# Attention and two feed-forward layers on one core: probability tiles, early loads and the spread of work on W in the first batch

## The chip, the cores and the metric

The kernel runs on one core of a Trainium2 chip. The metric is the device time of one execution in microseconds (us), lower is better. The kernel before takes 925.04 us, the median of three runs (924.96 to 925.62).

The core has engines with instruction streams of their own: PE (TensorE, matrix products and transposes through it; PEld is its loading of weights), DVE (VectorE), ACT (ScalarE), POOL (GpSimd) and SP (SyncE), which here issues all DMAs. Each works through its own stream in a fixed order and meets the others at semaphores.

## The reference

Windowed attention over 4 batches, 8 heads, 576 positions and head width 64, and behind it two feed-forward layers without a softmax or norm in between:

```python
def _attn_ref(q, k, v):                     # q, k, v: (4, 8, 576, 64)
    scores = scale * np.matmul(q, k.transpose(0, 1, 3, 2))
    mask = (rel >= 0) & (rel < 128)          # rel = query position - key position
    scores = np.where(mask, scores + slopes * -abs(rel), -1e9)
    attn = np.exp(scores - max)
    attn = attn / (sum(attn) + 1e-9)
    return np.matmul(attn, v)
x = attention, heads side by side            # (2304, 512)
h = ((x @ w1) * (x @ w2)) @ w3               # 512 -> 1024 -> 1024
y = h @ w_out                                # 1024 -> 512
h = y @ w_in                                 # 512 -> 2048
out = (h * clip(h + 3, 0, 6) / 6) @ v_out    # 2048 -> 512
```

## The kernel before

**Stages.** The first feed-forward layer uses the product W = w3 @ w_out, which the kernel makes itself while the attention of the first batch runs. After that come four batches of `ab` units (x @ w1 times x @ w2, line 464) and `y` units (times W, line 482), with the attention of the next batch between them, and then the second layer (`h_unit`, `o_unit`, lines 585 and 605). Products that need more than one pass are made of three matrix products of split operands (`mm3`, line 46).

**Attention.** It goes by head pairs n = 0 to 15, four to a batch. A pair takes six slots (`attn_slot`, line 304). Slot 0: the second head's product with v of the pair before (`pv(n - 1, 1)`), and the first two score tiles; slot 1: normalising these two, two more score tiles; slot 2: the fifth score tile (`j = 4`, the tail), normalising the rest; slot 3 and 4: transposes of the probabilities of the first and second head (`pt`), operands q and k of the next pair, loads of q and k for the pair behind it; slot 5: `pv(n, 0)`. A score tile j goes PE (line 193, or 195 and 196) to DVE (bias and row minimum, line 207) to ACT (exp, line 216) to DVE (1/sum, lines 224 and 225) to POOL (normalise, line 232) to PE (`pt`, lines 250 and 254), then ACT or DVE copies `th` (lines 260, 262) and PE multiplies by v (line 277). The result `xf` is split into `xh` and `xl` (line 298), which `ab` needs from all four pairs of the batch. Pairs 0 to 3 are "whole": q, k, v are used unsplit in buffers that alternate by `n % 2`; from pair 4 on they are split (`t_q`, `t_k`, `t_v`).

**Probability tiles.** Tiles `pr` of score tiles 0 to 3 come from one ring of four buffers (line 201), which is one pair's worth. The tail has one fixed tile `prt`. Ring `tl` of four buffers of the same size serves split pairs alone (line 241).

**Work on W.** w_out comes in four loads of 1 MB (`wo`), w3 in eight (`w3`), and w1 and w2 in eight (`w12`, f = 0 to 7). Each is unpacked by one ACT and two DVE instructions (`unpack`, lines 60 to 63). For each w3 load two halves of four products follow (`w_half`, line 389, tile `wps`), in unsplit f32, each product two instructions in the trace. `w12_unit` splits further (lines 69 and 70). Raw loads pass through three buffers, two in `rawp` and one in `rawx`. The list `work` (line 427) has 32 items: four `wo`, then each w3 with its two halves, with `w12` 0 to 3 ahead of the last three w3. Units `w12` 4 to 7 stand behind the whole list (lines 450 to 455), since their split tiles take the memory of unpacked w_out, and their loads reuse `rawp`.

**Order.** The program order of the first stage is the loop over 26 slots: `attn_slot(s)` and behind it the work items up to a share of the list:

```python
nslot = SLOTS * NP + 2          # 26
WEND = 6
upto = (s + 1) * len(work) // (nslot - WEND)
```

With `WEND = 6` all 32 items stand by slot 19, and slots 20 to 25 have attention alone. The order on each engine isn't this program order: the kernel is built with `schedule_with_timeline_sim=True` (line 694), and a planner fixes each engine's order beforehand, by its own estimate of when each instruction could run; among those it takes as ready, the one that stands first in the program goes first. On the chip that order is kept.

Of the kernel before, what the change touches and what calls it, by code (L numbers as in the profile page):

```python
# [8 lines left out]
F32 = mybir.dt.float32  # L9
# [8 lines left out]
P = 128  # L18
B, H, S, D = 4, 8, 576, 64
# [3 lines left out]
def tile_attention_moe_moe2(ctx: ExitStack, tc: tile.TileContext, qT, kT, vm, vt, wo, w3, w12, w2x, out):  # L23
# [7 lines left out]
    nc = tc.nc  # L31
# [6 lines left out]
    NHP = B * NP  # L38
# [51 lines left out]
    a1 = apool_ctx.enter_context(tc.tile_pool(name="a1", bufs=1, side="right"))  # L90
# [11 lines left out]
    def whole(n):  # L102
        return n < NWHOLE
# [2 lines left out]
    kw = [a1.tile([P, 2 * S], F32, tag=t, name=f"kw{t}") for t in ("rawk", "kh")]  # L106
    vw = [a1.tile([P, NC, P], F32, tag=t, name=f"vw{t}") for t in ("rawv", "vs")]
    rel8 = a1.tile([P, H, 2 * P], BF16, tag="kl", name="rel8")
    prt = a1.tile([P, 2 * P], F32, name="prt")
    sp1 = {}  # L110

    def split_tiles():
        if not sp1:
            sp1["rawq"] = a1.tile([P, 2 * S], F32, tag="rawq", name="rawq")
            sp1["rawk"] = a1.tile([P, 2 * S], F32, tag="rawk", name="rawk")
            sp1["rawv"] = a1.tile([P, NC, P], F32, tag="rawv", name="rawv")
            sp1["qs"] = a1.tile([P, SQ], F32R, tag="qs", name="qs")
            sp1["kh"] = a1.tile([P, 2 * S], F32R, tag="kh", name="kh")
            sp1["kl"] = a1.tile([P, 2 * S], F32R, tag="kl", name="kl")
            sp1["vs"] = a1.tile([P, NC, 2, P], F32R, tag="vs", name="vs")  # L120
            nc.gpsimd.memset(f32(sp1["qs"][:, 2 * S : SQ]), 0.0)
            nc.gpsimd.memset(sp1["rawv"][D:P, NC - 1, :], 0.0)
        return sp1

    def load_hp(n, names):
        for nm in names:
            if nm == "v":
                r = vw[n % 2] if whole(n) else split_tiles()["rawv"]
                nc.sync.dma_start(out=r[:, 0 : NC - 1, :], in_=vm[n])
                nc.sync.dma_start(out=r[0:TAIL, NC - 1, :], in_=vt[n])  # L130
                continue
            src = qT if nm == "q" else kT
            if whole(n):
                r = (qw if nm == "q" else kw)[n % 2]
            else:
                r = split_tiles()["raw" + nm]
            for a in range(1 if whole(n) else 2):
                nc.sync.dma_start(out=r[a * D : (a + 1) * D, 0 : 2 * S], in_=src[n])

    def slope(n, h):  # L140
        return 2.0 ** (-8.0 * (2 * (n % NP) + h + 1) / H)

    def t_q(n):

        if whole(n):
            return
        r, qs = split_tiles()["rawq"], split_tiles()["qs"]
        for h in range(2):
            sc = -(float(D) ** -0.5) / slope(n, h)
            c = slice(h * S, (h + 1) * S)  # L150
            nc.scalar.activation(qs[:, c], r[:, c], AF.Copy, scale=sc)
            nc.vector.scalar_tensor_tensor(
                out=qs[D:P, c], in0=r[D:P, c], scalar=sc, in1=f32(qs[D:P, c]), op0=ALU.mult, op1=ALU.subtract
            )
# [8 lines left out]
    def t_v(n):  # L163

        if whole(n):
            return
        t = split_tiles()
        r = t["rawv"].rearrange("p c (h d) -> p c h d", h=2)
        vs = t["vs"].rearrange("p c h (t d) -> p c h t d", t=2)
        for h in range(2):  # L170
            nc.vector.tensor_copy(vs[:, :, h, 0, :], r[:, :, h, :])
            nc.gpsimd.tensor_tensor(
                out=vs[:, :, h, 1, :], in0=r[:, :, h, :], in1=f32(vs[:, :, h, 0, :]), op=ALU.subtract
            )
# [6 lines left out]
    def scores(n, j):  # L181
        k0 = max(0, P * (j - 1))
        nk = min(S, P * (j + 1)) - k0
        mo = P if j == 0 else 0
        tail = j == NC - 1
        m = TAIL if tail else P
        ps = ps_s.tile([P, 2, 2 * P], F32, tag="s", name=f"s_{n}_{j}")
        for h in range(2):
            o = ps[:, h, 0:nk]
            qc = slice(h * S + P * j, h * S + P * (j + 1))  # L190
            kc = slice(h * S + k0, h * S + k0 + nk)
            if whole(n):
                nc.tensor.matmul(o, qw[n % 2][:, qc], kw[n % 2][:, kc], start=True, stop=True)
            else:
                nc.tensor.matmul(o, sp1["qs"][:, qc], sp1["kh"][:, kc], start=True, stop=False)
                nc.tensor.matmul(o, sp1["qs"][:, qc], sp1["kl"][:, kc], start=False, stop=True)

        if j == 0:
            stat[n] = [a1.tile([P, 2 * NC], F32, tag=t, bufs=2, name=f"{t}_{n}") for t in ("mn", "sm", "rc")]
        mn, sm, _ = stat[n]  # L200
        pr = prt if tail else a1.tile([P, 2, 2 * P], F32, tag="pr", bufs=4, name=f"pr_{n}_{j}")
        for h in range(2):
            a = h * m if tail else 0
            o = pr[a : a + m, 0:nk] if tail else pr[:, h, 0:nk]
            col = 2 * j + (0 if tail else h)

            nc.vector.tensor_tensor_reduce(
                out=o, in0=ps[0:m, h, 0:nk],
                in1=rel8[0:m, 2 * (n % NP) + h, mo : mo + nk] if whole(n) else relm[0:m, mo : mo + nk],
                op0=ALU.add, op1=ALU.min, scale=-(float(D) ** -0.5) if whole(n) else slope(n, h), scalar=3.0e38,  # L210
                accum_out=mn[a : a + m, col : col + 1],
            )
        for h in range(1 if tail else 2):
            o = pr[:, 0:nk] if tail else pr[:, h, 0:nk]
            col = 2 * j + h
            nc.scalar.activation(
                o, o, AF.Exp, bias=mn[:, col : col + 1], scale=-1.0, accum_out=sm[:, col : col + 1]
            )
        prob[n, j] = pr

    def normalize(n, js):
        _, sm, rc = stat[n]
        c0, c1 = 2 * js[0], min(2 * js[-1] + 2, 2 * NC - 1)
        nc.vector.tensor_scalar_add(rc[:, c0:c1], sm[:, c0:c1], 1e-9)
        nc.vector.reciprocal(rc[:, c0:c1], rc[:, c0:c1])  # L225
        for j in js:
            tail = j == NC - 1
            k0 = max(0, P * (j - 1))
            nk = min(S, P * (j + 1)) - k0
            for h in range(1 if tail else 2):  # L230
                o = prob[n, j][:, 0:nk] if tail else prob[n, j][:, h, 0:nk]
                nc.gpsimd.tensor_scalar(  # L232
                    out=o, in0=o, scalar1=rc[:, 2 * j + h : 2 * j + h + 1], scalar2=1.0, op0=ALU.mult, op1=ALU.mult
                )
# [69 lines left out]
    def attn_slot(g):  # L304
        n, s = divmod(g, SLOTS)
        ok = 0 <= n < NHP
        if s == 0:
            if 1 <= n <= NHP:
                pv(n - 1, 1)
            if ok:  # L310
                scores(n, 0)
                scores(n, 1)
        if not ok and not (s in (3, 4) and n == -1):
            return
        if s == 1:
            normalize(n, (0, 1))
            if n > 0 and whole(n - 1):
                load_hp(n, "v")
            scores(n, 2)
            scores(n, 3)  # L320
        elif s == 2:
            scores(n, 4)
            t_v(n)
            if n + 1 < NHP and not whole(n):
                load_hp(n + 1, "v")
            normalize(n, (2, 3, 4))
        elif s == 3:
            if ok:
                pt(n, 0, 0)
                pt(n, 0, 1)  # L330
            if n + 1 < NHP:
                t_q(n + 1)
                if n + 2 < NHP:
                    load_hp(n + 2, "q")
        elif s == 4:
            if ok:
                pt(n, 1, 0)
                pt(n, 1, 1)
            if n + 1 < NHP:
                t_k(n + 1)  # L340
                if n + 2 < NHP:
                    load_hp(n + 2, "k")
        elif s == 5:
            if ok:
                pv(n, 0)
# [60 lines left out]
    make_identity(nc, ident)  # L406
    for t in vw:
        nc.gpsimd.memset(t[D:P, NC - 1, :], 0.0)
    nc.gpsimd.memset(prt[:, P + D :], 0.0)
    nc.gpsimd.memset(three, 3.0)  # L410
    queue = [("wo", i) for i in range(KH)] + [("w3", i) for i in range(KF)]
    queue[-3:-3] = [("w12", f) for f in range(KH)]
# [2 lines left out]
    def more():  # L415
        nonlocal nxt
        if nxt < len(queue):
            k, i = queue[nxt]
            load((k, i), {"wo": wo, "w3": w3, "w12": w12}[k][i], rawp, rawp, rawx)
            nxt += 1  # L420

    more()
    load_hp(0, "v")
    more()
    load_hp(1, "qk")
    more()
    work = []
    for k, i in queue:
        work += [(k, i)] + ([("h", i, 0), ("h", i, 1)] if k == "w3" else [])
    nslot = SLOTS * NP + 2  # L430
    WEND = 6

    def do_work(w):
        if w[0] == "h":
# [7 lines left out]
    for s in range(nslot):  # L442
        attn_slot(s)
        upto = (s + 1) * len(work) // (nslot - WEND)
        if wi < len(work) and upto >= len(work):
# [253 lines left out]
```

## Time and profile before

| | us |
|---|---|
| median of three runs | 925.04 |
| the profiled execution, whole time | 920.97 |
| its span, first to last instruction | 919.1 |
| PE busy in it | 891.5 |

The profiled execution is 4.07 us faster than the median. All rows are from it; 1.87 us of its own time lie outside the span. Times of rows count from the span's start. In a timeline row the first two numbers are start and length of a merged run of instructions, and the bracket tells how long the engine was idle before it and what ended that. PE's lengths are modelled ends and overlap their successors.

### The profile page before, as it was taken

The page shows a single profiled execution, that of the slowest core. Times are in us where ns is not written, and L with a number is a line of the kernel's source. Part 1 is how long each engine was busy: PE and PEld are TensorE (multiplying, and loading weights), DVE is VectorE, ACT ScalarE, POOL GpSimd, SP SyncE. Part 2 cuts the span into 40 slices and gives each one's busy share as a digit, 9 for nine tenths or more (in the row PEclk, how much of TensorE's full clock was granted, in tenths as well). Part 3 has the DMA queues.
Part 4 walks back from the last instruction along what each step waited for, and adds up shares of the span by engine and source line. Part 5 has one row for each costly group of instructions (what it writes and reads, how often), then busy time and mean ns, then how long its engine had stood idle before and what let it go on. Part 6 is the DMA issues. An engine that isn't in the chain of part 4 may idle for free.

```text
span 919.1 us, 13413 instructions
## 1 busy us (share of the span) xinstructions
PE 891.5 (97%) x5216; PEld 782.5 (85%) x5216; DVE 439.6 (48%) x935; ACT 402.2 (44%) x856; POOL 152.0 (17%) x225
## 2 busy tenths in 40 slices
PE   5999889999999999999999999999999999999997
PEld 4555679999999999999899888888888888888896
DVE  5784767566664746554617683232223222322232
ACT  6664656565565635554416572232232222222232
POOL 4321323322232323230200010020001001000000
PEclk9999889999999999999999999999999999999999
DMA  9973422321322232103505651010001000100000
GB/s 290 357 267 115 157 66 65 80 68 48 84 73 59 66 85 66 39 2 117 185 27 188 234 200 47 0 69 1 1 0 46 1 1 1 46 1 1 15 32 24
DMA packets 23151, 74.00 MB, mean 81 GB/s; under 512 B 2864, under 2 KB 8496, under 8 KB 18480
## 3 DMA queue, kind: packets, MB, share of 16 engines
q1 hardware_dynamic: 23088, 73.15, 25.2%
q8 instruction: 41, 0.67, 0.3%
q14 instruction: 22, 0.18, 0.1%
HBM read 63.70 MB, written 9.44 MB: 80 GB/s over the span
## 4 chain that ended last, share of the span: by engine, by line
PE 89%; DMA 4%; DVE 3%; ACT 1%; issue 1%; POOL 1%; SPq 0%; DVEq 0%; ACTq 0%; POOLq 0%
PE o L47 7%; PE o L49 7%; PE o L48 7%; PE h L47 7%; PE h L48 7%; PE h L49 7%; PE ab L47 7%; PE ab L48 7%; PE ab L49 7%; PE wps L389 6%; PE X L277 4%; PE y L47 3%; PE y L48 3%; PE y L49 3%; DMA rawv<-in_w2x_dram 3%; PE pt L250 3%
## 5 line engine op out<-in xcount | busy, mean ns | idle before, releaser
L47 PE MATMUL ab<-xh,w12h 128*128 128x288 f32 x512 | 156.4, 306 | 5.0 <-ACT xh L69 3.1
L48 PE MATMUL ab<-xl,w12h 128*128 128x288 f32 x512 | 152.7, 298 | 0.0
L49 PE MATMUL ab<-xh,w12l 128*128 128x288 f32 x512 | 152.6, 298 | 0.0
L599 DVE SCALAR_TENSOR_TENSOR rl<-rl,h 128x512 f32<-128x512 f32 (+1 forms) x80 | 50.6, 634 | 208.7 <-ACT rl L598 208.7
L598 ACT ACTIVATE rl<-h,three 128x512 f32<-128x512 f32 (+1 forms) x80 | 51.6, 647 | 211.6 <-PE h L49 210.9
L47 PE MATMUL h<-yh,v2h 128*128 128x512 f32 (+1 forms) x320 | 118.5, 370 | 2.2 <-DVE rl L599 2.2
L49 PE MATMUL h<-yh,v2l 128*128 128x512 f32 (+1 forms) x320 | 118.1, 369 | 0.0
L48 PE MATMUL h<-yl,v2h 128*128 128x512 f32 (+1 forms) x320 | 117.9, 369 | 0.0
L47 PE MATMUL o<-v2h,g2h 128*128 128x512 f32 x288 | 112.9, 392 | 0.0
L48 PE MATMUL o<-v2l,g2h 128*128 128x512 f32 x288 | 112.3, 390 | 0.0
L49 PE MATMUL o<-v2h,g2l 128*128 128x512 f32 x288 | 111.4, 391 | 0.0
L47 PEld LDWEIGHTS ab<-xh,w12h 128*128 128x128 f32 x512 | 96.9, 190 | 7.1 <-ACT xh L69 3.5
L48 PEld LDWEIGHTS ab<-xl,w12h 128*128 128x128 f32 x512 | 97.5, 190 | 0.5 <-issue 0.2
L49 PEld LDWEIGHTS ab<-xh,w12l 128*128 128x128 f32 x512 | 97.3, 190 | 0.0
L232 POOL TENSOR_SCALAR pr<-pr,rc 128x256 f32<-128x256 f32 (+1 forms) x128 | 66.8, 541 | 153.6 <-DVE rc L225 77.5
L545 POOL TENSOR_TENSOR yl<-yraw,yh 128x1024 fp32r<-128x1024 f32 (+1 forms) x10 | 23.3, 2351 | 331.6 <-ACT yh L544 331.6
L70 DVE TENSOR_TENSOR g2l<-rl,g2h 128x512 fp32r<-128x512 f32 (+1 forms) x80 | 54.7, 684 | 47.3 <-ACT g2h L69 47.1
L47 PE MATMUL y<-g,Wh 128*128 128x288 f32 x256 | 75.6, 299 | 0.0
L48 PE MATMUL y<-g,Wh 128*128 128x288 f32 x256 | 75.4, 297 | 0.0
L49 PE MATMUL y<-g,Wl 128*128 128x288 f32 x256 | 75.0, 295 | 0.0
L47 PEld LDWEIGHTS h<-yh,v2h 128*128 128x128 f32 x320 | 60.1, 188 | 13.4 <-DVE rl L599 2.6
L48 PEld LDWEIGHTS h<-yl,v2h 128*128 128x128 f32 x320 | 60.1, 188 | 11.0
(106 smaller groups left out, 1645.9 us busy)
## 6 DMA issues: line engine op xcount, KB each, us to landing
raww<-in_w_dram SPq DMA_DIRECT2D x16, 1024.0 KB, 5.9
rawv<-in_w2x_dram SPq DMA_DIRECT2D x16, 1024.0 KB, 4.8
rawq<-in_qT_dram SPq DMA_DIRECT2D x24, 288.0 KB, 4.4
rawk<-in_kT_dram SPq DMA_DIRECT2D x24, 288.0 KB, 4.9
yT<-yf SPq DMA_DIRECT2D x32, 144.0 KB, 2.3
out_dram<-ob SPq DMA_DIRECT2D x18, 256.0 KB, 2.0
rawwo<-in_wo_dram SPq DMA_DIRECT2D x4, 1024.0 KB, 10.2
yraw<-yT SPq DMA_DIRECT2D x4, 1024.0 KB, 5.2
```

The costliest lines, as they stand in the source:

```text
L47: nc.tensor.matmul(ps, lh, rh, start=first, stop=False)
L48: nc.tensor.matmul(ps, lh, rl, start=False, stop=False)
L49: nc.tensor.matmul(ps, ll, rh, start=False, stop=last)
L70: lo_eng.tensor_tensor(out=lo, in0=src, in1=f32(hi), op=ALU.subtract)
L232: nc.gpsimd.tensor_scalar(out=o, in0=o, scalar1=rc[:, 2 * j + h : 2 * j + h + 1], scalar2=1.0, op0=ALU.mult, op1=ALU.mult)
L250: nc.tensor.transpose(ps[:, o : o + P], prob[n, j][:, h, c : c + P], ident)
L277: nc.tensor.matmul(X[:, c0 : c0 + nq], l, r, start=bank not in seen, stop=last[bank] == idx, skip_group_check=True)
L389: nc.tensor.matmul(ps[:, 0:DM], w3v[i][:, m, :], wov[m], start=m == 0, stop=m == KF - 1)
L545: nc.gpsimd.tensor_tensor(out=yl[:, c, 0:n], in0=t[:, c, 0:n], in1=f32(yh[:, c, 0:n]), op=ALU.subtract)
L598: nc.scalar.activation(rl[:, 0:n], ps[:, 0:n], AF.Relu, bias=three[:, 0:1], scale=1.0)
L599: nc.vector.scalar_tensor_tensor(out=rl[:, 0:n], in0=rl[:, 0:n], scalar=6.0, in1=ps[:, 0:n], op0=ALU.min, op1=ALU.mult)
```

## The change

- **Probability tiles.** `prt` becomes two tiles, taken by `n % 2`. The `pr` tiles of odd whole pairs (1 and 3) come from ring `tl`, the others from ring `pr`.
- **v.** v of a whole pair n + 1 is loaded in slot 1 of pair n, instead of slot 1 of pair n + 1. v of pair 4 is loaded in slot 2 of pair 3, instead of slot 1 of pair 4. Later pairs as before.
- **First loads.** The order was q0 k0, wo 0, v0, wo 1, q1 k1, wo 2 and becomes q0 k0, v0, wo 0, q1 k1, wo 1, wo 2.
- **Work on W.** `WEND` goes from 6 to 0: the 32 items are spread over all 26 slots, and units `w12` 4 to 7 stand behind slot 25.
- One more memset on POOL, for the second `prt`.

```diff
-    prt = a1.tile([P, 2 * P], F32, name="prt")
+    prt = [a1.tile([P, 2 * P], F32, name=f"prt{i}") for i in range(2)]
...
-        pr = prt if tail else a1.tile([P, 2, 2 * P], F32, tag="pr", bufs=4, name=f"pr_{n}_{j}")
+        ring = "tl" if whole(n) and n % 2 else "pr"
+        pr = prt[n % 2] if tail else a1.tile([P, 2, 2 * P], F32, tag=ring, bufs=4, name=f"pr_{n}_{j}")
...
             normalize(n, (0, 1))
-            if n > 0 and whole(n - 1):
-                load_hp(n, "v")
+            if n + 1 < NHP and whole(n + 1):
+                load_hp(n + 1, "v")
...
             t_v(n)
-            if n + 1 < NHP and not whole(n):
+            if n + 1 < NHP and not whole(n + 1):
                 load_hp(n + 1, "v")
...
-    nc.gpsimd.memset(prt[:, P + D :], 0.0)
+    for t in prt:
+        nc.gpsimd.memset(t[:, P + D :], 0.0)
...
-    more()
     load_hp(0, "v")
     more()
     load_hp(1, "qk")
+    more()
     more()
...
-    WEND = 6
+    WEND = 0
```

## Rows read from the trace of the kernel before

**Rows 1.** The page: span, PE's busy share, PE and its granted clock in 40 slices.
```profile
span 919.1 us, 13413 instructions
PE 891.5 (97%) x5216; PEld 782.5 (85%) x5216; DVE 439.6 (48%) x935; ACT 402.2 (44%) x856; POOL 152.0 (17%) x225
...
PE   5999889999999999999999999999999999999997
...
PEclk9999889999999999999999999999999999999999
```

**Rows 2.** Busy time by stretch: length, busy and instructions of each engine, granted clock, DMA share, GB/s.
```profile
core 0: us, PE busy (x) PEld busy (x) DVE busy (x) ACT busy (x) POOL busy (x), PEclk, DMA share, GB/s
30.53:102.04 71.51, 71.51 (x237) 39.62 (x238) 49.22 (x90) 39.35 (x65) 19.12 (x22) 1.00 0.64 230
102.04:130.02 27.98, 20.01 (x95) 16.18 (x94) 21.11 (x51) 16.06 (x44) 9.86 (x16) 0.80 0.28 76
130.02:135.00 4.98, 4.97 (x30) 4.62 (x30) 1.73 (x3) 1.72 (x4) 2.06 (x5) 0.77 0.80 171
140.00:160.00 20.00, 20.00 (x159) 20.00 (x159) 13.61 (x35) 12.04 (x30) 8.65 (x13) 1.00 0.29 75
240.00:260.00 20.00, 20.00 (x160) 20.00 (x160) 14.16 (x42) 12.70 (x33) 7.42 (x13) 1.00 0.30 75
```

**Rows 3.** PE timeline around the products for W: the first, a scores row, the last.
```profile
25.43 0.61 PE L193 MATMUL s<-kwrawk,qwrawq 128*128 128x128 f32 x4
...
30.53 7.13 PE L389 MATMUL wps<-wov,w3v 128*128 128x512 f32 x16
...
95.43 2.79 PE L389 MATMUL wps<-wov,w3v 128*128 128x512 f32 x6
```

**Rows 4.** PE timeline behind them: rows with a wait, and the last product with v.
```profile
103.92 2.18 PE L277 MATMUL X<-th,vwrawv 128*128 128x64 f32 x12 [1.23 <-ACT xf L286]
...
108.89 0.85 PE L47 MATMUL ab<-xh,w12h 128*128 128x288 f32 x2 [1.78 <-ACT xh L69]
...
121.60 2.18 PE L277 MATMUL X<-th,vwvs 128*128 128x64 f32 x12
...
126.05 0.53 PE L47 MATMUL ab<-xh,w12h 128*128 128x288 f32 x2 [1.34 <-ACT xh L69]
...
129.58 0.44 PE L48 MATMUL ab<-xl,w12h 128*128 128x288 f32 x1
```

**Rows 5.** PE and ACT timelines of the first 31 us: rows that wait for a load.
```profile
15.72 2.43 PE L193 MATMUL s<-kwkh,qwqs 128*128 128x128 f32 x8 [3.62 <-DMA kwkh<-in_kT_dram]
...
18.26 1.18 ACT L60 ACTIVATE rawwo<-rawwo 128x1024 f32<-128x1024 f32 x1 [3.19 <-DMA rawwo<-in_wo_dram]
```

**Rows 6.** Busy time by stretch, columns as in rows 2, of four earlier stretches.
```profile
6.00:18.00 12.00, 8.11 (x29) 6.38 (x30) 7.47 (x28) 8.24 (x26) 2.90 (x5) 0.93 1.02 338
18.00:30.53 12.53, 11.43 (x65) 9.39 (x63) 10.63 (x31) 9.17 (x24) 5.43 (x9) 0.93 1.04 332
40.00:60.00 20.00, 20.00 (x59) 9.71 (x58) 18.12 (x29) 12.94 (x21) 6.15 (x4) 1.00 0.74 277
60.00:80.00 20.00, 20.00 (x70) 11.70 (x69) 14.66 (x28) 11.32 (x21) 2.55 (x5) 1.00 0.72 248
```

**Rows 7.** POOL timeline: four normalisings of one pair, at two times.
```profile
49.33 6.15 POOL L232 TENSOR_SCALAR pr<-pr,rc 128x128 f32<-128x128 f32 x4 [10.34 <-ACT raww L60]
...
117.90 1.64 POOL L232 TENSOR_SCALAR pr<-pr,rc 128x128 f32<-128x128 f32 x4 [3.67 <-DVE rc L225]
```

**Rows 8.** DVE timeline: the last two units w12, and the last split of the batch.
```profile
97.56 0.70 DVE L61 TENSOR_SCALAR raww<-raww 128x1024 int32<-128x1024 int32 x1 [0.46 <-DMA raww<-in_w_dram]
98.85 1.23 DVE L63 SCALAR_TENSOR_TENSOR raww<-raww 128x1024 int32<-128x1024 int32 x1 [0.59 <-ACT raww L60]
...
101.89 1.22 DVE L70 TENSOR_TENSOR w12l<-raww,w12h 128x1024 fp32r<-128x1024 f32 x1
...
109.12 1.84 DVE L70 TENSOR_TENSOR w12l<-raww,w12h 128x1024 fp32r<-128x1024 f32 x1
...
128.75 0.82 DVE L70 TENSOR_TENSOR xl<-xf,xh 128x288 fp32r<-128x288 f32 x2
```

**Rows 9.** SP timeline: issues of pair 3's v and of the last two loads of w12.
```profile
72.02 0.33 SPq L129 DMA_DIRECT2D vwvs<-in_vm_dram  x1
...
92.91 2.39 SPq L358 DMA_DIRECT2D raww<-in_w_dram  x2
```

## The prediction

> **What bounds the kernel now.** I read the page first. PE is busy for 97% of the span, in 40 slices nearly always at 9, and its granted clock dips in slices 5 and 6, some 92 to 138 us [rows 1]. So time can be won only where PE isn't fed: in the first slices and around 110 us. The table of stretches shows the second place [rows 2]. From 30.53 to 102.04 PE has work without a break. From 102.04 to 130.02 it runs 95 instructions in 27.98 us, with a mean clock of 0.80, and from 130.02 to 135.00 it runs 30 at 0.77. In a full stretch it runs 160 in 20.00 us, 0.125 us each, and the two full stretches shown agree within one instruction. They hold nearly the same kinds of products as the thin stretch, so I use 0.125 us as the price of one.
>
> The PE timeline says why the stretch is thin. The products for W run from 30.53 to 98.22 and then there are none left [rows 3]. What follows is the attention of pair 3 and the start of pair 4, one step after another. PE waits for `xf`, then for `xh`, then again for `xh` [rows 4], and the first ab product that needs pair 3's `xl` starts at 129.58. The rows in between carry no single long wait: it is a chain through DVE, ACT and POOL with nothing to put beside it on PE. The clock belongs to the same loss. PE works sparsely from 102 on, and a mean of 0.80 between full and half means that some 40% of the stretch ran at the lower level, 1.2 GHz, where each product takes longer.
>
> **The change part by part.**
>
> *Work on W in all 26 slots.* This removes no instruction and adds none. It moves W items behind attention in the planner's preference: at slot 17, say, 28 of the 32 items stood before and 22 stand after. That the planner does run things far from their place is seen in rows 3: scores of pair 2, program slot 12, run at 25.43, ahead of the first product for W, slot 3. So W work fills whatever PE time attention leaves, in both kernels. What differs is who goes first where both are ready. Before, W went first and was used up at 98; now pair 3 goes first and the last two halves stand in slot 25, behind `pv(3, 1)` in slot 24. The gain is the lost time of the thin stretch. 95 instructions at 0.125 are 11.9 us, so 16.1 of the 27.98 us are lost; 30 at 0.125 are 3.75, so 1.2 of the next 4.98 are lost. Together **17.3 us** [rows 2].
>
> Of this something stays. (a) The handover: the last product with v ends at 123.78, and the first ab product that has all it needs starts at 129.58, 5.8 us later [rows 4]. The two halves behind it cover 7.13 us of PE, measured for one pair of halves [rows 3], unless the planner has pulled them forward. Bounds 0 and 5.8; I take 2.0, as most of the cover should remain. (b) Units `w12` 4 to 7 now stand just ahead of the first ab unit and can't finish before the last product for W, whose operands hold their memory. A unit costs DVE 0.70 + 1.23 + 1.22 = 3.15 us [rows 8]. Two of the four loads have their buffers early; the last two were issued at 92.91 [rows 9], and their units ended at 103.11 and 110.96 [rows 8], the later one 12.7 us after the last product. An ab unit is 24 products, 3.0 us, so unit 4 is wanted 12.0 us after ab starts and unit 7 after 21: in time. But two units are 6.3 us on DVE beside ab and the next batch's attention, which leave DVE 5.84 of 20 us [rows 2], about 6.1 in 21 us. That just fits. Bounds 0 and 6.3; I take 1.5.
>
> *Two sets of probability tiles, second `prt`.* Nothing is executed for them but one small memset on POOL ahead of ACT's first copies; that has slack, since pair 0's scores wait for a load. What goes is a wait: DVE's first step of pair n + 1 no longer waits until PE has transposed pair n. Ring `tl` is needed for its old use only from pair 4's transposes on, behind pair 3's in any order. Cost 0.
>
> *First loads.* q1 and k1 now go ahead of one more 1 MB load. DMA is full there, 338 GB/s [rows 6], so 1.05 MB is 3.1 us. PE waited 3.62 us for k1 at 15.72 [rows 5], and with its own tiles pair 1 can use that time. In return `wo` 1 lands later by q1 and k1, 0.59 MB or 1.7 us, and `wo` 0 by v0, about 0.9. The total ahead of the first w3 load is the same, and while the queue is full its landing and the first product at 30.53 stay. ACT stands 3.19 us waiting for `wo` 2 with exps behind it [rows 5]; how the planner orders that again is not to be seen. Bounds: 0, and 3.1 us gained; I take 1.0.
>
> *v one pair earlier.* Each load is two issues on SP. Its tile comes free with the `pv` in the slot ahead, so it can wait there and hold back weight loads queued behind it on SP. Pair 3's v was issued at 72.02, just as the products with v that release its tile ended, so it goes no earlier than that [rows 9]. One w3 load feeds about 7 us of PE and three buffers are in turn, so a wait of a few us is covered. Taken as 0.
>
> Sum: 17.3 + 1.0 - 2.0 - 1.5 = **14.8 us**. After 130 us PE is full until the second layer, so the whole shift reaches the end. Against the profiled execution, 920.97, that is 906.2. The median is 4.07 higher, and I put the same saving on it: 925.04 - 14.8 = **910.2**. The bounds of the terms give 17.3 + 3.1 = 20.4 at best (904.6) and 17.3 - 5.8 - 6.3 = 5.2 at worst (919.8).
>
> **The rivals.**
>
> *DVE and POOL hold attention back.* Where W work is dense, attention's small steps take longer. Four normalisings took 6.15 us at 49.33, with DVE busy for 18.12 of 20 us around them, and 1.64 at 117.90, when W work was over [rows 6, 7]. The Trainium skill ("SBUF — State Buffer", its glossary entry on the shared port pair) says that DVE and GpSimd lock one pair of ports for a whole instruction and the loser blocks. It speaks against this change, since the normalisings of pairs 2 and 3 move in among W's DVE work, and the two rows agree with it. To judge the effect on time, count DVE: it works 49.22 + 21.11 + 1.73 = 72.1 us between 30.53 and 135.00 [rows 2]. My forecast wants that in 87.2 us, a share of 0.83. It reached 0.91 in one stretch but 0.73 in the next [rows 6]. At 0.73 the same work lasts until about 129, a saving of 6.2 us, 918.8.
>
> *The change doesn't do what it says.* If attention is seldom ready in the planner's picture, W is pulled forward just as before, is used up near 98, and the thin stretch stays. Then only the early 1.0 us is left: 924.0. Against it: with two tile sets and earlier q, k and v, attention is ready sooner, and W's own pace is bound to PE.
>
> *Slower: waits inside the full stretch.* Each engine's order is fixed ahead. Before, attention came between long runs of W products, and 71.51 us passed without a wait. Now its steps, each behind a chain through four engines, alternate with W more finely. If the planner takes such a chain as shorter than it is, PE stands at a transpose with ready W products queued behind it. Some 18 slots lie in that stretch, so from 17.3 / 18 = 0.96 us per slot on the gain is eaten; at 1.5 us it is 27 - 17.3 = 9.7 us slower, 934.7. For it: POOL's spread from 1.64 to 6.15 us, which no fixed plan can foresee [rows 7]. Against it: from 18.00 to 30.53 three pairs were mixed without W, and PE was still busy for 11.43 of 12.53 us [rows 6].
>
> **How the numbers follow.** My forecast 0.63, 910.2 us; DVE and POOL as a bound 0.20, 918.8; no effect 0.08, 924.0; slower 0.09, 934.7. The range 904 to 920 takes in the bounds of the terms and the first rival, and leaves out the other two and a little, under 2 in 10. A measurement of this kernel tells about 0.2%, 1.9 us, from no change: faster below 923.2, slower above 926.9. So faster 0.63 + 0.20 = 0.83, same 0.08, slower 0.09.
>
> **What would show it.** In the changed kernel's profile the last product for W should end between 105 and 112, with `pv(3, 1)` ahead of it; the granted clock should stay full from 31 us on; PE should run about 160 instructions per 20 us from 120 at the latest. Waits of PE on POOL `pr` or ACT `th` inside 31 to 105 would speak for the slower rival; an ab wait on `w12h` or on DVE `asb` for term (b); a wait on `xh` behind the last W product for term (a). The prediction is wrong if the W products again end near 98 with attention still to come, or if PE's stretches after 140 lose their 160 per 20 us.

## The result and the profile after

The changed kernel takes 918.17 us (median of 4 runs, 915.40 to 919.37) beside 925.33 (4 runs, 924.96 to 925.79): a ratio of 0.991, 95% interval 0.988 to 0.994, so 7.2 us less. The sign is as forecast and the time lies in the range, but the saving is half of the forecast 14.8. A second comparison, with the experiments, gave 914.72 beside 924.70 (4 and 15 runs), ratio 0.990 (0.987 to 0.992), 10.0 us less, which is still short of the forecast.

> The changed kernel once more, as the measure for the three beside it on the same chip. 917 to 919 us.

The two intervals overlap; the working below goes by the first comparison and the traces.

The profiled execution of after is its fastest run, 915.40 us, 5.57 less than that of before. Its page, to be read beside [rows 1]:

```profile
span 913.6 us, 13395 instructions
...
PE 887.4 (97%) x5216; PEld 780.2 (85%) x5216; DVE 436.4 (48%) x935; ACT 401.5 (44%) x856; POOL 148.1 (16%) x226
...
PE   5899979999999999999999999999999999999998
...
PEclk9999989999999999999999999999999999999999
```

There is still a dip, in slice 6 (some 114 to 137 us), but the clock dips in one slice instead of two. The same instructions run on PE; only their order differs. Busy time by stretch, columns as in [rows 2], from the last product for W on:

```profile
core 0: us, PE busy (x) PEld busy (x) DVE busy (x) ACT busy (x) POOL busy (x), PEclk, DMA share, GB/s
104.53:122.36 17.83, 12.10 (x76) 10.46 (x74) 15.98 (x30) 10.81 (x21) 2.21 (x2) 0.91 0.41 138
122.36:140.00 17.64, 17.64 (x126) 17.50 (x127) 9.77 (x37) 9.61 (x27) 4.77 (x10) 0.90 0.18 46
...
140.00:160.00 20.00, 20.00 (x160) 20.00 (x159) 14.61 (x41) 13.17 (x39) 7.28 (x13) 1.00 0.31 75
```

At the prediction's price of 0.125 us an instruction, 76 are 9.5 us, so 8.3 of the first 17.83 us are lost; 126 are 15.75, so 1.9 of the next 17.64 are lost. That makes 10.2 us lost where before lost 17.3 [rows 2], so 7.1 less. From 140 on PE is as full as before. The change therefore works where the forecast put it; but 10.2 us stay where 2.0 + 1.5 = 3.5 were forecast.

The traces bear out the count up to 435 us, but the lead doesn't reach the end whole. PE timelines, before and then after: the one wait of an ab product for DVE's `asb`, and the first product of the second layer.

```profile
442.48 0.40 PE L47 MATMUL ab<-xh,w12h 128*128 128x288 f32 x1 [1.60 <-DVE asb L478]
...
445.77 0.40 PE L47 MATMUL h<-yh,v2h 128*128 128x512 f32 x1
```

```profile
435.68 0.40 PE L47 MATMUL ab<-xh,w12h 128*128 128x288 f32 x1 [1.77 <-DVE asb L480]
...
440.48 0.40 PE L47 MATMUL h<-yh,v2h 128*128 128x512 f32 x1
```

The first is 6.8 us earlier in after, the second only 5.3. In between the granted clock of after fell, to a mean of 0.57 from 436 to 440 us (length, PE busy, clock, DMA share, GB/s):

```profile
436.00:440.00 4.00, 4.00 (x21) 0.57 0.34 68
```

Before kept 1.00 from 440 to 460 us, behind the same wait, and so did the other profiled execution of after (914.53 us) from 436 to 440. So the two executions end 5.57 us apart in whole time, and that the count of 7.1 lies so near the 7.2 of the medians is in part luck.

The PE timeline of after: the first scores of pair 1, the first and the last products for W, pair 3's last product with v, and the first ab product with its `xl`.

```profile
12.56 0.68 PE L193 MATMUL s<-kwkh,qwqs 128*128 128x128 f32 x4 [0.35 <-DMA kwkh<-in_kT_dram]
...
34.42 7.03 PE L390 MATMUL wps<-wov,w3v 128*128 128x512 f32 x16
...
98.36 6.17 PE L390 MATMUL wps<-wov,w3v 128*128 128x512 f32 x14
...
104.48 0.60 PE L251 MATMUL pt<-ident,pr 128*128 128x128 f32 x4
...
112.48 2.18 PE L278 MATMUL X<-th,vwvs 128*128 128x64 f32 x12 [1.03 <-ACT xf L287]
118.02 0.47 PE L195 MATMUL s<-kh,qs 128*128 128x128 f32 x2 [3.37 <-DVE qs L152]
...
122.36 0.61 PE L48 MATMUL ab<-xl,w12h 128*128 128x288 f32 x1 [0.47 <-DVE xl L70]
```

The last product for W now ends at 104.53 (before 98.22), and pair 3's last product with v ends 10.1 us behind it, at 114.66; before it was 25.6 us behind, at 123.78 [rows 4]. The first ab product with pair 3's `xl` starts 7.2 us earlier, at 122.36 instead of 129.58. Where the 8.3 us go, the same table for PE alone tells (length, PE busy, clock, DMA share, GB/s):

```profile
core 0: us, PE busy (x), PEclk, DMA share, GB/s
104.53:114.66 10.13, 9.10 (x65) 1.00 0.47 175
114.66:122.36 7.70, 3.01 (x11) 0.79 0.34 90
```

Up to the end of pair 3 PE loses 10.1 - 65 x 0.125 = 2.0 us. In the handover behind it, 11 instructions run in 7.70 us, and 6.3 us are lost.

### The profile page after: what moved, and what is told of

Read it like the earlier page. It is cut to its first block, busy times and chain, and to the rows that moved or that the text cites. A ratio compares the mean times of both kernels' runs of the same rounds, so it can differ in the third digit from the quotient of the medians.

```text
span 913.6 us, 13395 instructions
## 1 busy us (share of the span) xinstructions
PE 887.4 (97%) x5216; PEld 780.2 (85%) x5216; DVE 436.4 (48%) x935; ACT 401.5 (44%) x856; POOL 148.1 (16%) x226
## 3 DMA queue, kind: packets, MB, share of 16 engines
q1 hardware_dynamic: 23088, 73.15, 25.6%
## 4 chain that ended last, share of the span: by engine, by line
PE 87%; DMA 5%; DVE 4%; ACT 1%; issue 1%; POOL 1%; SPq 0%; DVEq 0%; ACTq 0%; POOLq 0%
PE o L47 7%; PE o L49 7%; PE o L48 7%; PE h L47 7%; PE h L49 7%; PE h L48 7%; PE ab L47 7%; PE ab L48 7%; PE ab L49 6%; PE wps L390 6%; PE X L278 4%; DMA rawv<-in_w2x_dram 3%; PE y L47 3%; PE y L48 3%; PE y L49 3%; PE pt L251 2%
## 5 line engine op out<-in xcount | busy, mean ns | idle before, releaser
L47 PEld LDWEIGHTS ab<-xh,w12h 128*128 128x128 f32 x512 | 97.6, 191 | 3.6 <-DVE asb L480 2.2
```

The lines of the kernel that those rows point to most:

```text
L47: nc.tensor.matmul(ps, lh, rh, start=first, stop=False)
```

## The experiments

### Which part makes the gain

The forecast gave nearly all of the gain to the spread of the work on W and none to the tiles. Five kernels take the parts apart. Where nothing else is said they ran beside 27 runs of before on one chip (median 926.22).

**W alone**: the kernel before with one number changed.

```diff
-    WEND = 6
+    WEND = 0
```

> The kernel before with the work on W spread over all 26 slots (WEND = 0) and nothing else. Theory 'order of W': the spread makes nearly all of the gain, 6 to 7 us, so 918 to 919 us, with the last product for W near 104 and the first ab product with pair 3's xl near 123. Theory 'tiles': with one ring, pair n + 1 can't go ahead of pair n's transposes, so attention isn't ready earlier and W is still pulled forward: 923 to 925 us, last product for W near 99.

Measured: 926.24 us (10 runs), ratio 0.9998 (0.998 to 1.002). The spread alone does nothing. Products for W end at 102.59, 4.4 us later than before, but they also start 4.3 us later (34.85 beside 30.53) and take 67.7 us in both; pair 3's last product with v moves with them, to 127.51, 24.9 us behind. The DVE timeline of this kernel says what holds pair 3, the first step on its scores, and the PE timeline has these scores and transposes of pair 2:

```profile
97.66 0.29 DVE L207 CUSTOM_DVE_ANT_0 pr<-s,rel 128x128 f32<-128x128 f32 x1 [0.41 <-PE pt L250]
```

```profile
77.35 0.61 PE L193 MATMUL s<-kwkh,qwqs 128*128 128x128 f32 x4
...
97.24 0.93 PE L250 MATMUL pt<-ident,pr 128*128 128x128 f32 x7
```

The scores were ready at 78 us. The DVE row shows only 0.41 us of waiting because the step stands that late in DVE's order. DVE writes the result into a `pr` tile, there is one ring of four, and these are held until PE has transposed pair 2. That pair 3 stands ahead of W in the program is then worth nothing: it isn't ready. In after, with a ring for odd pairs, the same step runs 60 us earlier, and pair 4's first step as soon as its scores are there:

```profile
37.04 0.28 DVE L208 CUSTOM_DVE_ANT_0 pr<-s,rel 128x128 f32<-128x128 f32 x1
...
96.73 0.29 DVE L208 CUSTOM_DVE_ANT_0 pr<-s,relm 128x128 f32<-128x128 f32 x1 [3.17 <-PE s L196]
```

**The change without the spread of W**: after, with the old number.

```diff
-    WEND = 0
+    WEND = 6
```

> The changed kernel with WEND = 6 again: two tile sets, early v and the new first loads, without the spread of W. Theory 'order of W': 924 to 925 us, thin stretch from about 100 to 129 as before. Theory 'tiles': 919 to 921 us, because attention now runs ahead by itself and the thin stretch is shorter.

Measured: 923.04 us (10 runs), ratio 0.9974 (0.9944 to 1.0004). That is 2.4 us by the ratio, anything from nothing to 5.2 by its interval, so a part of the gain at most. The spread is needed too.

**Tiles alone**: the kernel before with the two sets of tiles.

```diff
-    prt = a1.tile([P, 2 * P], F32, name="prt")
+    prt = [a1.tile([P, 2 * P], F32, name=f"prt{i}") for i in range(2)]
...
-        pr = prt if tail else a1.tile([P, 2, 2 * P], F32, tag="pr", bufs=4, name=f"pr_{n}_{j}")
+        ring = "tl" if whole(n) and n % 2 else "pr"
+        pr = prt[n % 2] if tail else a1.tile([P, 2, 2 * P], F32, tag=ring, bufs=4, name=f"pr_{n}_{j}")
...
-    nc.gpsimd.memset(prt[:, P + D :], 0.0)
+    for t in prt:
+        nc.gpsimd.memset(t[:, P + D :], 0.0)
```

> The kernel before with the two tile sets alone. Theory 'order of W': no change, 924.5 to 925.5 us. Theory 'tiles': 920 to 923 us.

Measured: 923.35 us (10 runs), ratio 0.9954 (0.9924 to 0.9984), a gain of 4.3 us by the ratio and 2.9 by the medians, which just stands out.

**Tiles and W together**: the whole edit of tiles alone and that of W alone, on the kernel before with its loads of v and its first loads.

```diff
-    prt = a1.tile([P, 2 * P], F32, name="prt")
+    prt = [a1.tile([P, 2 * P], F32, name=f"prt{i}") for i in range(2)]
...
-    WEND = 6
+    WEND = 0
```

> The kernel before with the two tile sets and the spread of W, without the early v and without the new first loads. Theory 'tiles and spread need each other' (the spread alone gave nothing, the tiles alone a part): these two are the whole gain, 917 to 919 us, pair 3's last product with v near 115. If the early v is needed too, because pv of a pair waits for it: 920 to 923 us, with PE waiting at pv for v.

Measured, beside 15 runs of before: 918.47 us (10 runs) against 924.70, ratio 0.993 (0.991 to 0.995). That is 6.2 us, where the whole change gained 10.0 in the same comparison: most of the gain, and by the intervals, which overlap, perhaps all of it. The markers of the profiled executions, in us; "pair 3 behind W" is the end of pair 3's last product with v minus the end of the last W product, and the last column is the start of the split minus the start of the first product for W:

| kernel | last W product ends | pair 3's last product with v ends | first product for W | pair 3 behind W | first DVE split `xl` of pair 3 | `xl` behind W's start |
|---|---|---|---|---|---|---|
| before | 98.22 | 123.78 | 30.53 | 25.6 | 128.75 | 98.2 |
| W alone | 102.59 | 127.51 | 34.85 | 24.9 | 132.48 | 97.6 |
| without W | 101.99 | 128.54 | 34.30 | 26.6 | 131.29 | 97.0 |
| tiles alone | 100.59 | 125.36 | 32.84 | 24.8 | 127.04 | 94.2 |
| tiles and W | 111.63 | 122.24 | 40.15 | 10.6 | 128.34 | 88.2 |
| after | 104.53 | 114.66 | 34.42 | 10.1 | 121.85 | 87.4 |

Only the two together take pair 3 from 25 us behind W to 10. What the spread adds once the tiles are there is seen in the tail scores of pair 3 and what follows from them. First tiles alone, PE and POOL timelines:

```profile
100.43 0.81 PE L193 MATMUL s<-kwkh,qwqs 128*128 128x192 f32 x4
...
113.28 0.69 PE L251 MATMUL pt<-ident,pr 128*128 128x128 f32 x2 [1.22 <-POOL pr L233]
```

```profile
110.83 3.77 POOL L233 TENSOR_SCALAR pr<-pr,rc 128x256 f32<-128x256 f32 x4 [9.36 <-DVE rc L226]
```

Then tiles and W, where W's products run until 111.63:

```profile
93.65 0.81 PE L193 MATMUL s<-kwkh,qwqs 128*128 128x192 f32 x4
...
103.70 0.38 PE L251 MATMUL pt<-ident,pr 128*128 128x128 f32 x2
```

```profile
100.00 1.84 POOL L233 TENSOR_SCALAR pr<-pr,rc 128x256 f32<-128x256 f32 x4 [5.32 <-DVE rc L226]
```

With the old order of W all its products go ahead of pair 3's tail scores (the last ends at 100.59, the scores start at 100.43), and what follows is again a chain with nothing beside it: normalising from 110.83, transposes from 113.28. With the spread the tail scores stand 18 us ahead of the end of W, and normalising and the first transposes pass under its products.

The lost time by the count used above puts the kernels in about the order of their times. Busy time of PE from the last product for W on, one row of each kernel (W alone, tiles alone, tiles and W):

```profile
102.59:150.00 47.41, 38.64 (x229) 0.86 0.28 77
```

```profile
100.59:145.00 44.41, 36.04 (x230) 0.85 0.36 106
```

```profile
111.63:150.00 38.37, 33.54 (x219) 0.87 0.28 86
```

Lost are 47.41 - 28.6 = 18.8 us, 44.41 - 28.75 = 15.7 and 38.37 - 27.4 = 11.0, beside 17.3 before and 10.2 after. Against before that is 1.5 more, 1.6 less and 6.3 less, where the medians have 0.0, 2.9 and 6.2 less.

**The old order of the first loads**, in after.

```diff
+    more()
     load_hp(0, "v")
     more()
     load_hp(1, "qk")
     more()
-    more()
```

> The changed kernel with the first loads in the old order (wo 0, v0, wo 1, q1 k1, wo 2). In the changed kernel the first product for W starts at 34.4 instead of 30.5 us, with attention run in between. If the new order of loads costs W a later start that is never won back, the old order brings the start to about 31 and saves 2 to 3 us: 915 to 916 us. If the new order is worth the 1.0 us of the prediction: 919 to 920 us, with PE's 3.6 us wait for pair 1's k back.

Measured: 917.33 us (6 runs), ratio 0.990 (0.987 to 0.993), as with the new order. PE's wait for k1 did shrink in after, from 3.62 us [rows 5] to 0.35, but the time won there isn't to be seen at the end. W's first product came at 34.42 instead of 30.53: the rest of pair 2's scores, more of pair 1's transposes and pair 3's first scores now run ahead of it, and PE waits there 4.3 us in all for POOL's normalising, where before it waited 0.7.

### Where the missing half is

By the table above 6.3 of the 10.2 us that stay are the handover from pair 3 to ab. The prediction thought the last two halves of W would lie under it. In after they don't: the run of products that ends at 104.53 stands ahead of pair 3's last transposes (104.48), as the prediction's "unless" said.

**W further back in the program.**

```diff
-    WEND = 0
+    WEND = -6
...
-        upto = (s + 1) * len(work) // (nslot - WEND)
+        upto = (s + 1) * len(work) // (nslot - WEND) if s < nslot - 1 else len(work)
```

> The changed kernel with W spread still thinner (WEND = -6, the last six items behind slot 25). In the changed kernel W ends at 104.5 us and pair 3's attention at 114.7, so W is still used up 10 us too soon. If that is W's place in the program, thinner W moves W's end past 107 and pair 3's end before 113: 914 to 916 us. If the planner pulls W into whatever gaps attention's own pace leaves, as in the run of the spread alone, the two ends stay within 2 us: 917 to 919 us.

Measured: 917.28 us (6 runs), ratio 0.992 (0.990 to 0.995), no gain on after, which took 914.72 beside it. W's last product still ends 10.1 us ahead of pair 3's (107.37 and 117.45). Standing last in the program doesn't put it last on PE: where the planner sees PE free it pulls W forward.

**Other work off DVE.** During the handover DVE has a queue of its own. Its timeline in after, from pair 3's last product with v on:

```profile
115.10 0.76 DVE L289 COPY xf<-X 64x576 f32<-64x576 f32 x1
115.90 0.62 DVE L171 CAST vs<-rawv 128x320 fp32r<-128x320 f32 x2
116.55 1.33 DVE L152 SCALAR_TENSOR_TENSOR qs<-rawq,qs 64x576 fp32r<-64x576 f32 x1
117.91 1.91 DVE L70 TENSOR_TENSOR kl<-rawk,kh 128x1152 fp32r<-128x1152 f32 x1
119.85 0.76 DVE L152 SCALAR_TENSOR_TENSOR qs<-rawq,qs 64x576 fp32r<-64x576 f32 x1
120.64 1.23 DVE L70 TENSOR_TENSOR w12l<-raww,w12h 128x1024 fp32r<-128x1024 f32 x1
...
121.85 0.82 DVE L70 TENSOR_TENSOR xl<-xf,xh 128x288 fp32r<-128x288 f32 x2
```

Between `xf`, ready at 115.86, and the split `xl` at 121.85 stand operands of later pairs and the last `w12` unit. ACT has a like queue ahead of `xh`, which it makes at 118.02. So `xl` and the last two `w12` splits were put on POOL.

```diff
-                split(xh, xl, x[:, s * HS : (s + 1) * HS], nc.vector if n == NP - 1 else nc.gpsimd)
+                split(xh, xl, x[:, s * HS : (s + 1) * HS], nc.gpsimd)
...
-        split(flat(hi), flat(lo), unpack(rawt.pop(("w12", f))), nc.vector)
+        split(flat(hi), flat(lo), unpack(rawt.pop(("w12", f))), nc.gpsimd if f >= KH + 2 else nc.vector)
```

> The changed kernel with pair 3's xl and the lo parts of units w12 6 and 7 made on POOL instead of DVE. In the changed kernel DVE made xf at 115.9 and xl only at 121.9, with the operands of pair 5 and a w12 part in between, and POOL idle. If this crowd on DVE is what costs the handover, the first product that needs xl starts 4 to 5 us earlier: 913 to 915 us. If DVE's crowd only stands there because nothing better was ready: 917 to 919 us.

Measured: 916.35 us (4 runs), ratio 0.992 (0.989 to 0.995), no gain. POOL's timeline, and a row of PE's:

```profile
119.51 3.51 POOL L70 TENSOR_TENSOR w12l<-raww,w12h 128x1024 fp32r<-128x1024 f32 x1
122.99 2.08 POOL L70 TENSOR_TENSOR xl<-xf,xh 128x288 fp32r<-128x288 f32 x2
```

```profile
118.97 0.47 PE L195 MATMUL s<-kh,qs 128*128 128x128 f32 x2 [3.29 <-DVE qs L152]
```

The `w12` split takes 3.51 us on POOL where DVE takes 1.23, so `xl` comes no earlier, and PE stands at pair 5's scores as before, 3.29 us instead of 3.37. The chain behind this wait holds no `w12` split: after pair 3's last product DVE makes `xf`, `vs` and then the `qs` that PE waits for. For `xl` the run decides nothing, since POOL's queue took the place of DVE's.

**Pair 5's operands later.** PE's longest wait there is for pair 5's `qs`. Here the program loads q and k of pair 5 in slot 25 instead of slots 21 and 22.

```diff
             if n + 1 < NHP and whole(n + 1):
                 load_hp(n + 1, "v")
+            if n == NP:
+                load_hp(n + 1, "qk")
...
-                if n + 2 < NHP:
+                if n + 2 < NHP and n != NP - 1:
                     load_hp(n + 2, "q")
...
-                if n + 2 < NHP:
+                if n + 2 < NHP and n != NP - 1:
                     load_hp(n + 2, "k")
```

> The changed kernel with q and k of pair 5 loaded in slot 25 instead of slots 21 and 22, so that their splitting on ACT and DVE can't stand in front of pair 3's xh and xl, nor pair 5's scores in front of the ab products on PE. If this crowd makes the handover long, it falls from 7.7 to 4 to 5 us: ratio to before 0.986 to 0.989. If the handover is set elsewhere, ratio 0.989 to 0.993.

Measured: 915.38 us (4 runs) beside 924.04, ratio 0.991 (0.989 to 0.993), no gain on after. But on the chip the loads didn't move against the work around them. SP issued pair 5's k, in after and then here, at

```profile
91.56 1.10 SPq L138 DMA_DIRECT2D rawk<-in_kT_dram  x2
```

```profile
95.35 1.10 SPq L138 DMA_DIRECT2D rawk<-in_kT_dram  x2
```

and DVE had ended its split of pair 4's k, which stood in the same tile, at 91.53 and 95.32: in both kernels the load goes as soon as its tile is free, over 20 us before pair 5's `qs`. Pair 3's last product with v ends at 117.41 and its `xl` starts at 124.62, 7.2 us later as in after, and PE waits 3.38 us for pair 5's `qs` all the same. What a later load would do is therefore not tested.

**The last two halves held behind pair 3.** Here the missing cover is put there by hand: the last two halves of W may be issued on PE only behind `pv(3, 1)`.

```diff
+    pv_end = {}
...
-            nc.tensor.matmul(
+            mm = nc.tensor.matmul(
...
+        pv_end[n, h] = mm
...
+        if w[0] == "h" and w[1:] in ((KF - 1, 0), (KF - 1, 1)):
+            with tc.issue_after(pv_end[NP - 1, 1].ins):
+                w_half(w[1], w[2])
+            return
```

> The changed kernel with the last two halves of W held behind pair 3's last product with v in PE's order, where the prediction had put them. In the changed kernel they ran from 98.4 to 104.5 us, in front of pair 3's last transposes, and the handover from 114.7 to 122.4 had no cover. If the uncovered handover is the missing part of the gain, pair 3's end comes about 5 us earlier (109 to 110), W fills the handover, and the first product with pair 3's xl starts at 117 to 119: 4 to 5 us faster than the changed kernel, ratio to before 0.985 to 0.988. Rival: attention's own pace through DVE and POOL sets pair 3's end, or units w12 4 to 7, which wait for W's end, then stop the ab units: ratio 0.989 to 0.993 as for the changed kernel.

Measured: 913.90 us (4 runs, 913.39 to 916.79), ratio 0.990 (0.988 to 0.993), not to be told from after. The handover itself is repaired: pair 3's last product with v ends at 109.37, W at 116.73 behind it, and `xl` is split at 110.81, 1.4 us behind the product instead of 7.2. But a new gap opens, seen in the busy time by stretch of this kernel, with the columns of the stretches of after:

```profile
120.00:130.00 10.00, 10.00 (x79) 9.79 (x78) 9.50 (x20) 9.11 (x19) 0.00 (x0) 1.00 0.11 46
130.00:140.00 10.00, 7.53 (x54) 6.56 (x53) 9.80 (x27) 7.22 (x20) 5.60 (x6) 1.00 0.20 54
140.00:150.00 10.00, 10.00 (x81) 10.00 (x80) 6.29 (x21) 6.44 (x19) 4.19 (x8) 1.00 0.41 95
```

From 120 to 140 DVE is busy for 19.3 of 20 us, and from 130 PE runs 54 instructions, 6.75 us worth, so 3.25 us are lost again. PE stands idle there for DVE, 1.07 us for pair 4's `xf` (the row below) and 1.0 us for pair 6's `qs`, and 0.33 us for POOL.

```profile
132.81 0.27 PE L279 MATMUL X<-th,vs 128*128 128x64 f32 x1 [1.07 <-DVE xf L294]
```

Both edits at once, holding W and loading pair 5 later, gave the same.

> Both edits together. If both theories hold, W covers most of a shorter handover and the first product with xl starts at about 117: ratio to before 0.983 to 0.986. If only the cover counts, the same as the run that holds W.

Measured: 915.81 us (4 runs), ratio 0.991 (0.989 to 0.994). Pair 5's loads didn't move here either (k at 93.22 us, beside 92.93 with W held alone), so this run tells no more than the one with W held.

**Held, with four splits off DVE.** If DVE's load makes the new gap, it should go when the splits of `w12` 4 to 7 move to POOL; the halves are held as above.

```diff
-        split(flat(hi), flat(lo), unpack(rawt.pop(("w12", f))), nc.vector)
+        split(flat(hi), flat(lo), unpack(rawt.pop(("w12", f))), nc.gpsimd if f >= KH else nc.vector)
```

> The run that holds W, with the lo parts of units w12 4 to 7 made on POOL instead of DVE. With W held, the gap moved: PE ran 54 instructions from 130 to 140 us, DVE was busy for 9.80 of the 10 us, and POOL was idle from 112.7 to 132.0. If DVE's load is now the bound, taking its w12 lo parts away (1.22 us each) raises the 54 to 65 or more: ratio to before 0.985 to 0.988. If the order on DVE counts and not its load, or POOL's copies (2.4 us each beside DVE) come too late for ab units 4 to 7, the ratio stays at 0.990 or rises.

Measured: 916.26 us (6 runs) beside 924.53, ratio 0.991 (0.989 to 0.993). No gain, and the gap is deeper, in the same view:

```profile
130.00:140.00 10.00, 7.78 (x40) 6.58 (x39) 8.83 (x14) 6.67 (x18) 5.63 (x7) 0.75 0.31 84
```

DVE has 1.0 us less to do, but PE runs 40 instructions instead of 54, at a lower clock. The wait for `qs` is gone and that for `xf` is 0.92 us, but a wait for POOL has come up. PE's row and POOL's:

```profile
132.66 0.33 PE L252 MATMUL pt<-ident,pr 128*128 128x128 f32 x1 [1.22 <-POOL pr L234]
```

```profile
129.79 2.43 POOL L70 TENSOR_TENSOR w12l<-raww,w12h 128x1024 fp32r<-128x1024 f32 x1 [1.05 <-ACT w12h L69]
132.18 1.68 POOL L234 TENSOR_SCALAR pr<-pr,rc 128x128 f32<-128x128 f32 x4
```

POOL took 2.97 and 2.43 us for two of these splits, and the second stands right ahead of the normalising that PE waits for. So the edit moved part of the wait from DVE to POOL, and it doesn't tell whether DVE's load or the order of its queue makes the gap. This stays open. None of the versions beats the changed kernel by more than the measurement tells.

## Why the prediction was right and wrong

**Where the time is won: right.** The gain lies in the thin stretch behind the products for W, the price of 0.125 us an instruction accounts for it (17.3 - 10.2 = 7.1 beside a lead of 6.8 us in the traces at 435 us). That "the whole shift reaches the end" the traces don't show: the profiled execution of after lost 1.5 us of its lead to a fall of the clock behind 436.

**Who wins it: wrong.** The step "*Two sets of probability tiles* ... What goes is a wait ... Cost 0" failed, together with "What differs is who goes first where both are ready". W alone gave 0.0 us, tiles alone 2.9 by the medians (4.3 by the ratio), both 6.2. The prediction named the wait that goes and gave it no worth in its sum, although against its second rival it leaned on the tiles ("with two tile sets and earlier q, k and v, attention is ready sooner"). It should have asked what it holds back: with one ring pair 3 isn't ready before pair 2 is transposed at 93 to 97 us, so putting it ahead of W in the program changes nothing. That the sign and the place came out right all the same is luck in so far as the change happens to make both edits; as an account of W alone the 17.3 us were wrong.

**Term (a), the handover: mis-sized.** Put at 2.0 us within bounds 0 to 5.8; 6.3 us are lost there, beyond the upper bound, because the handover also grew from 5.8 to 7.70 us. This makes 4.3 of the missing 7.6 us. The mechanism was named in the text ("unless the planner has pulled them forward"), but the value leaned on the place in the program, when rows 3 had just been read as showing that the planner runs things far from their place.

**The rest of the stretch: left out.** 2.0 us go between the end of W and the end of pair 3, where the prediction had no term, since it took `pv(3, 1)` to lie ahead of the last products for W. 1.9 us go between 122.36 and 140, near the 1.5 of term (b), but not for its reason: PE has no wait for `w12h` there, and its only wait for DVE's `asb` is the one at 435.68. PE is without a gap there, at a mean clock of 0.90. (The term's own sum was a little tight: 6.3 us of work don't fit into 6.1.) Together these are (2.0 + 1.9) - 1.5 = 2.4 us more than forecast.

**The first loads: not seen.** 1.0 us was put on them; undoing them changed nothing that can be measured. 4.3 + 2.4 + 1.0 = 7.7 us, which is the gap of 7.6 but for rounding; by the second comparison the gap is only 14.8 - 10.0 = 4.8, so the shares hold for the traced execution. v one pair earlier was taken as 0. Tiles and W, which lacks it and the new first loads, took 918.47 beside 914.72 for after in the same comparison, with overlapping intervals. After with the old first loads, which has v, had a ratio of 0.990 beside 0.993 for tiles and W, with overlapping intervals again, and in the trace of tiles and W PE never waits for v. Whether v has a part in these 3.8 us stays open.

**The rivals.** The time of the first comparison came nearest to the first, DVE and POOL holding attention back (918.8), and so did its measure: between 34.42 and 122.36 DVE was busy for 50.01 + 15.98 = 66.0 of 87.94 us, a share of 0.75, where the rival had 0.73 and the forecast wanted 0.83. But a share isn't a bound. PE was busy throughout the first 70 us of this, and moving splits off DVE gained nothing, though they took longer on POOL; what stays is one gap, the handover, and how far the pace of DVE and POOL sets its length no run separates from the order of their queues. Of the page of the Trainium skill that the rival named ("SBUF — State Buffer", the glossary entry on the shared port pair) this much is seen: four normalisings of 128x128 took 3.06 us at 73.58 in after, with W running, between the 1.64 and 6.15 of [rows 7], and one split of 128x1024 took 2.40 to 3.51 us on POOL. Which engine held the ports no run here tells.

The slower rival didn't show: the list of PE's waits in after has none from 34.42 to 104.53. That the change does nothing is what W alone did.

**What would show it.** The last product for W ended at 104.53, just short of 105 to 112, and with pair 3's end behind it, not ahead: that sign alone told that the cover was missing. The granted clock stayed full up to the end of pair 3 and fell to a mean of 0.79 behind it. 160 instructions in 20 us are reached from 140, not from 120.

## What to carry to other kernels

Two edits that each open a different gate can be worth little or nothing one by one and most of the gain together, so ask of each part not only what it costs but which later work it lets start, and of each reordering whether the work that is put first is ready by then. Where a planner fixes the order, a place at the end of the program is no promise: read from the trace what it has pulled forward (here the last halves of W, and the loads of pair 5 that an edit was to delay), and take work as cover for a gap only if something holds it there. And a gap that is filled by hand can come back one step later, as here between 130 and 140 us, so read next which queue feeds the stage behind it.

## What the runs showed of the hardware

The first loads don't always come at the same rate. Busy time from 6 to 24 us, where DMA is full in every execution: first after, then tiles and W.

```profile
6.00:24.00 18.00, 14.69 (x65) 11.28 (x66) 13.38 (x57) 15.32 (x51) 8.37 (x13) 1.00 1.02 340
```

```profile
6.00:24.00 18.00, 11.09 (x39) 8.85 (x39) 9.42 (x41) 11.08 (x34) 1.79 (x5) 0.81 1.03 274
```

340 and 274 GB/s for much the same loads; W alone had 284, before 335, tiles alone 346. With the slow start the first product for W came at 40.15 instead of 34.42 us, which moves everything behind it. Tiles and W, W alone, before and tiles alone all have the same order of first loads, so this looks like a spread between executions and not between kernels; what makes it no run tells. The times spread as well: 27 runs of before on one chip went from 919.9 to 930.2 us, and the ten of tiles and W from 913.35 to 921.65, the profiled one with the slow start being the slowest of them. The loads aren't all of it, since the profiled run of W alone, with 284 GB/s, was faster than its median, and the clock differs too: from 522 to 530 us its mean was 0.79 in the traces of four of the experiments and 1.00 in the others. A difference of 2 or 3 us between two single executions therefore says little here. Counted from the first product for W the traces agree better: pair 3's `xl` lies 87.4 us behind it in after and 88.2 in tiles and W.
